# Order of the second network's mix units, and GpSimd casts for fourteen split rows, in an attention, maxout and PReLU kernel

## The chip, the cores and the metric

One Trainium2 chip, of which the kernel uses one core. The metric is device time in microseconds (us) of one execution. The kernel before was timed in three runs. One further execution was profiled, and all rows below come from that one. TensorE is called PE, VectorE DVE, ScalarE ACT, GpSimd POOL, and the engine that issues every DMA here is SyncE, SP.

## What is computed

```python
# attention: B, H, S, D = 4, 8, 576, 64; heads 0-3 see the last 32 positions, heads 4-7 every 32nd
attn = softmax(where(mask, q @ k.T / 8, -1e9)); x = (attn @ v) as rows        # (2304, 512)
h = maximum(maximum(x @ w1, x @ w2), x @ w3); x2 = h @ w_out                  # 512 -> 768 -> 512
h = x2 @ w_in; g = maximum(h, 0) + alpha * minimum(h, 0); out = g @ w_out2    # 512 -> 2048 -> 512
```

The texts call the first network (maxout) "the network" of a batch entry `b`: there are four, b = 0 to 3, each of 576 rows in two halves of 288 (`HALF`). "The second woven network" is that of b = 1. "The second net" of the diff's `split_x2`, the PReLU one, is called the output network here, to keep the two apart; it runs over three blocks of 768 rows, each in two parts of 384 (`HB`).

## The kernel before

All products run in fp32r as high part and low part: a value is cast to its high part and the rest becomes the low part (`split`, L236), and three matmuls replace one (`PAIRS`).

**Weave.** Attention for all four entries, the conversion of all weights and the networks of b = 0, 1, 2 are entered as tasks of a `Weave` (L53). A list planner on the host (`plan`) orders them: a task has a due position `pos`, what it needs, and ring buffers that it takes (8 PSUM banks, 10 tiles `x`, 4 tiles `t`, 12 tiles `h`); among the tasks that could start within 120 ns of the earliest on the engine that is free first, the one with the smallest position goes. The outcome is one fixed order of instructions for each engine. A network has 44 units on PE: 36 gate units of 12 matmuls (L752), three for each of six column groups and two halves, and 8 mix units of 18 matmuls (L777), four for each half. `units` turns a list into that order, and `net_tasks(b, list)` gives unit n the position 44 b + n. A mix unit needs the six `h` tiles of its half (high and low part), writes through one bank, an ACT copy (L823) and a `t` tile to DRAM (`store_x2`, L786). In a list, a pair is a group of three gate units and `None` stands for four mix units. The attention of entry b + 1 is woven under the network of b: scores (L358 local, L474 strided), transposes (L403, L523), values (L432, L547), whose results go into `x` tiles. The ring of `x` holds 10 tiles, an entry needs 8.

**Last network.** `last_net(3)` (from 291.5 us) is written out by hand. Twelve gate units come first, then 42 products of L932 (six groups k = 3 to 8 of seven, a Strassen-Winograd form) whose results DVE adds up (L912), one in seven being copied by ACT first (L950), then 8 mix units. In every third group (g = 2) each result gets a last maximum on DVE, an ACT cast (L945) and a DVE subtraction (L919) to become `h`.

**Early splits.** Block 1 of the output network needs 7 combinations of its rows for each of two halves of the columns, as high and low part in DRAM (`xd`). They are made inside `last_net`: step n of its loop emits `early_split` for n = 10, 12, ..., 22 (half 0) and n = 32, 34, ..., 44 (half 1). Each takes a tile of two pools of two buffers (`xst`, `xsu`, in turn), casts its 128x384 high part on ACT, subtracts on POOL (both L239/L242), and `early_store` issues the store at the step after. The sums that half 1 is split from are made by POOL (L1017, step 30), those of half 0 by DVE.

SP works its list in order: stores, then loads of the next factors (L865), of the rows of block 0 (`load_x2`, L1008, steps 45 and 47), of the output network's weights (L1060, L1072). DVE sums and splits block 0 (L1017, L242 at 354 to 366 us), and from 366.87 us PE runs the output network (L1401, L1202, L1208, L1212).

Due lists before:

```python
    GATES = [(0, 0), (0, 1), (0, 2), (1, 0), (0, 3), (0, 4), (1, 1), (0, 5), (1, 2),
             None, (1, 3), (1, 4), (1, 5), None]
    GATES_THEN = [what for what in GATES if what] + [None, None]
```

Of the kernel before, what the change touches and what calls it, by code (L numbers as in the profile page):

```python
# [57 lines left out]
class Weave:  # L58
# [16 lines left out]
    def add(self, engines, emit, pos, needs=(), gives=(), makes=(), uses=(), mode=None, slack=0, small=0):  # L75
        t = len(self.tasks)
        if engines[0][0] != "PE" and any(key in self.banks for key in uses):
            pos -= self.URGENT
        self.banks.update(key for ring, key in makes if ring == "bank")
        self.tasks.append((engines, emit, pos, needs, makes, mode, slack, small))  # L80
        for ring, key in makes:
            if ring in self.order:
                self.order[ring].append(key)
        for e in gives:
            self.givers.setdefault(e, []).append(t)
            if e[0] == "stored":
                self.stores.add(t)
        for key in [key for _, key in makes] + list(uses):
            self.users.setdefault(key, []).append(t)
# [89 lines left out]
def attention_maxout_prelu_kernel(  # L179
# [13 lines left out]
    nc = tc.nc  # L193
# [43 lines left out]
    def split(hi, lo, src, hi_engine, lo_engine):  # L237
        if hi_engine is nc.scalar:
            hi_engine.copy(hi, src)  # L239
        else:  # L240
            hi_engine.tensor_copy(hi, src)
        lo_engine.tensor_tensor(out=lo, in0=src, in1=hi.bitcast(F32), op=ALU.subtract)  # L242
# [5 lines left out]
    def pool(stack, name, bufs, side="left"):  # L248
        return stack.enter_context(tc.tile_pool(name=name, bufs=bufs, side=side, reuse_waits="tile"))
# [41 lines left out]
    def sub(out_, x, y):  # L291
        nc.vector.tensor_tensor(out=out_, in0=x, in1=y, op=ALU.subtract)  # L292

    def act(n, chip=False):
        return ("ACT", (50 if chip else 100) + 5 * n // 6)

    def dve(n, ops=1):
        return ("DVE", ops * (75 + 21 * n // 20))

    def load(kb):  # L300
        return (("SP", 3 * kb),)
# [443 lines left out]
    def gate_products(b, hf, f, g):  # L745
        acc = bank()
        unread(acc, UNREAD.get((b, hf, f, g), 0))
        acc = acc[:, :HALF]
        n = 0
        for cc in gate_order:  # L750
            for wi, xi in PAIRS:
                nc.tensor.matmul(acc, words["gate", f, g][:, wi, cc * P:(cc + 1) * P],  # L752
                                 xt[b, cc, hf][:, xi, :], start=n == 0, stop=n == 3 * NCC - 1)
                n += 1
        return acc
# [13 lines left out]
    def out1_products(b, hf, dc, st):  # L769
        acc = bank()[:, :HALF]  # L770
        out1_part(acc, hf, dc, st, range(NF1))
        return acc
# [7 lines left out]
    def store_x2(b, hf, dc, xo):  # L780
        first = b * S + hf * HALF
        done = 0
        while done < HALF:
            i, s = divmod(first + done, HB)
            nn = min(HALF - done, HB - s)
            nc.sync.dma_start(x2d[i][:, dc, s:s + nn], xo[:, done:done + nn])  # L786
            done += nn
# [3 lines left out]
    GATES_FIRST = [(0, 0), (0, 1), (1, 0), (0, 2), (1, 1), (0, 3), (1, 2), (0, 4), (1, 3), (0, 5),  # L791
                   (1, 4), None, (1, 5), None]
# [3 lines that stand above are left out]
    GATES_LAST = [(0, 0), (1, 0), (1, 1), (0, 1)]  # L796

    def units(gates):
        hf = 0
        for what in gates:  # L800
            if what is None:
                yield from ((hf, None, dc) for dc in range(NCC))
                hf += 1
            else:
                yield from ((*what, g) for g in range(3))

    def net_tasks(b, gates):
        sts = {}
        for n, (hf, f, g) in enumerate(units(gates)):
            pos = b * NUNITS + n  # L810
            u = (b, hf, f, g)
            ak = ("acc", u)
            if f is None:
                xok = ("xo", u)

                def products(_, hf=hf, dc=g, ak=ak, xok=xok):
                    tl[xok] = tp.tile([P, HALF], F32, tag="t", name="xo")
                    tl[ak] = out1_products(b, hf, dc, {("h", hf, f): tl["h", b, hf, f] for f in range(NF1)})

                hks = [("h", b, hf, f) for f in range(NF1)]  # L820
                add((("PE", 3 * NF1 * 132),), products, pos, needs=hks + [("mix", f) for f in range(NF1)],
                    gives=[ak], makes=[("bank", ak), ("t", xok)], uses=hks, mode="products")
                add((act(HALF, True),), lambda _, ak=ak, xok=xok: nc.scalar.copy(tl[xok], tl[ak]),  # L823
                    pos, needs=[ak], gives=[xok], uses=[ak, xok])
                add(load(144), lambda _, hf=hf, dc=g, xok=xok: store_x2(b, hf, dc, tl[xok]), pos,
                    needs=[xok], gives=[("x2", u)], uses=[xok])
                continue
            tk, hk = ("t", b, hf, f), ("h", b, hf, f)
            xks = [("x", b, cc, hf) for cc in range(NCC)]

            def products(_, hf=hf, f=f, g=g, ak=ak, tk=tk):
                if g == 0:
                    tl[tk] = tp.tile([P, HALF], F32, tag="t", name="t")
                tl[ak] = gate_products(b, hf, f, g)

            add((("PE", 3 * NCC * 132),), products, pos, gives=[ak, ("begun", g, tk)],
                needs=xks + [("gate", f, g)] + ([("begun", g - 1, tk)] if g else []),
                makes=[("bank", ak)] + ([("t", tk)] if g == 0 else []), uses=xks, mode="products")
            if g == 0:
                add((act(HALF, True),), lambda _, ak=ak, tk=tk: nc.scalar.copy(tl[tk], tl[ak]), pos,  # L840
                    needs=[ak], gives=[("t0", tk)], uses=[ak, tk])
            else:
                add((dve(HALF),), lambda _, ak=ak, tk=tk: nc.vector.tensor_tensor(  # L843
                    out=tl[tk], in0=tl[ak], in1=tl[tk], op=ALU.max), pos,
                    needs=[ak, (f"t{g - 1}", tk)], gives=[(f"t{g}", tk)], uses=[ak, tk])
            if g == 2:
                def high(_, tk=tk, hk=hk):
                    h = tl[hk] = hp.tile([P, 2, HALF], F32R, tag="x", name="h")
                    nc.scalar.copy(h[:, 0], tl[tk])

                add((act(HALF),), high, pos - 40, needs=[("t2", tk)], gives=[("hhi", hk)],
                    makes=[("h", hk)], uses=[tk])
                add((dve(HALF),), lambda _, tk=tk, hk=hk: sub(tl[hk][:, 1], tl[tk],
                                                              tl[hk][:, 0].bitcast(F32)),
                    pos - 40, needs=[("hhi", hk)], gives=[hk], uses=[tk, hk])

    def last_net(b):
# [130 lines left out]
        for hf in range(2):  # L988
            for dc in range(NCC):
# [9 lines left out]
    PRODUCTS = (((0, 0), "11"), ((2, 256), "T2"), ((0, 256), "21"), ((2, 0), "T3"),  # L999
                ((1, 0), "T1"), ((1, 256), "T4"), ((3, 0), "22"))  # L1000
    xs, x2h = {}, {}
# [22 lines left out]
                        ("T3", t3), ("T4", t4)):  # L1024
            xs[blk, name, i] = x

    def split_x2(blk, k, i, pool, tag, lo_engine=nc.vector):

        t = pool.tile([P, 2, HB], F32R, tag=tag, name=tag)
        split(t[:, 0], t[:, 1], xs.pop((blk, PRODUCTS[k][1], i)), nc.scalar, lo_engine)  # L1030
        return t

    early_rows, early_parts = {}, []
# [5 lines left out]
        sum_x2(blk, i, early_rows.pop((blk, i)), engine, later)  # L1039

    def early_split(blk, i, k, pool=None):
        early_parts.append((blk, k, i, split_x2(blk, k, i, pool or xst, "xst", nc.gpsimd)))

    def early_store():
        for blk, k, i, t in early_parts:
# [69 lines left out]
    for _, tasks, args in sorted(late, key=lambda it: it[0]):  # L1115
        tasks(*args)
    for b in range(B - 1):
        net_tasks(b, (GATES_FIRST, GATES, GATES_THEN)[b])
    weave.run()
    nc.sync.dma_start(alpha_sb, alpha)  # L1120
    conv_x.close()
# [4 lines left out]
    xst = pool(ctx, "xst", 2, "right")  # L1126
# [365 lines left out]
    for n in range(NQ * NBLK):  # L1492
        blk, q = divmod(n, NQ)
# [72 lines left out]
```

## Time and profile before

| | us |
|---|---|
| median of three runs | 726.78 |
| lowest and highest | 726.24, 728.15 |
| profiled execution | 727.66 |
| its span | 725.8 |
| outside the span (727.66 - 725.8) | 1.9 |

The profile gives busy time by engine, a table by stretch (busy time of each engine in a window of the span), the list of waits, the timeline of an engine (start and length of merged runs of equal instructions, with the idle time ahead of them and what ended it), the chain of waits (what the end of the program goes back to, piece by piece) and the DMAs (size, and time from issue to landing). A line such as `t<-bank,t` names what an instruction writes and reads. PE's ends are modelled, so a loss on PE is read from starts, and from the idle time in brackets.

### The profile page before, as it was taken

The page shows a single profiled execution, that of the slowest core. Times are in us where ns is not written, and L with a number is a line of the kernel's source. Part 1 is how long each engine was busy: PE and PEld are TensorE (multiplying, and loading weights), DVE is VectorE, ACT ScalarE, POOL GpSimd, SP SyncE. Part 2 cuts the span into 40 slices and gives each one's busy share as a digit, 9 for nine tenths or more (in the row PEclk, how much of TensorE's full clock was granted, in tenths as well). Part 3 has the DMA queues.
Part 4 walks back from the last instruction along what each step waited for, and adds up shares of the span by engine and source line. Part 5 has one row for each costly group of instructions (what it writes and reads, how often), then busy time and mean ns, then how long its engine had stood idle before and what let it go on. Part 6 is the DMA issues. An engine that isn't in the chain of part 4 may idle for free.

```text
span 725.8 us, 18183 instructions
## 1 busy us (share of the span) xinstructions
PE 714.3 (98%) x6682; PEld 696.4 (96%) x6682; DVE 619.1 (85%) x1689; ACT 443.2 (61%) x1175; POOL 25.6 (4%) x49
## 2 busy tenths in 40 slices
PE   8899999999999999999999999999999999999998
PEld 5799999999999999999999999999999999999997
DVE  6989886898989897679878988979988888888896
ACT  6879975977767484243356566535666644656561
POOL 2000000000000000045000000000000000000000
PEclk9999999999999999999999999999999999999999
DMA  8776599898999879698989899999789999878362
GB/s 298 268 259 229 174 334 314 312 315 307 345 339 324 279 250 321 204 351 294 326 322 400 274 330 340 403 386 360 245 301 329 372 402 344 295 233 259 113 190 77
DMA packets 90089, 214.46 MB, mean 295 GB/s; under 512 B 11152, under 2 KB 41360, under 8 KB 90000
## 3 DMA queue, kind: packets, MB, share of 16 engines
q1 hardware_dynamic: 90000, 213.30, 83.8%
q8 instruction: 53, 0.87, 0.5%
q14 instruction: 36, 0.29, 0.1%
HBM read 157.16 MB, written 56.10 MB: 294 GB/s over the span
## 4 chain that ended last, share of the span: by engine, by line
PE 92%; DMA 3%; ACT 2%; DVE 2%; issue 1%; POOL 0%; SPq 0%; DVEq 0%; POOLq 0%; ACTq 0%
PE bank L752 26%; PE ph L1401 24%; PE po L1202 15%; PE bank L777 10%; PE po L1208 4%; PE ph L1202 4%; PE po L1212 2%; PE bank L932 2%; PE bank L432 1%; DVE t L912 1%; DMA xd<-xst 1%; PE bank L358 1%; ACT e L374 1%; PE bank L474 1%; DMA w<-ws 1%; DMA k<-in_kTs 1%
## 5 line engine op out<-in xcount | busy, mean ns | idle before, releaser
L1401 PE MATMUL ph<-x,w 128*128 128x384 f32 x990 | 199.4, 336 | 0.0
L752 PE MATMUL bank<-x,w 128*128 128x288 f32 x1440 | 197.0, 297 | 1.2 <-ACT w L289 0.8
L752 PEld LDWEIGHTS bank<-x,w 128*128 128x128 f32 x1440 | 191.6, 189 | 2.7 <-ACT w L289 1.2
L1401 PEld LDWEIGHTS ph<-x,w 128*128 128x128 f32 x990 | 166.6, 188 | 0.8
L1202 PE MATMUL po<-w,g 128*128 128x256 f32 x936 | 135.9, 282 | 0.0
L1202 PEld LDWEIGHTS po<-w,g 128*128 128x128 f32 x936 | 130.1, 190 | 0.3
L1407 DVE TENSOR_TENSOR c<-ph,c 128x384 f32<-128x384 f32 x165 | 89.4, 554 | 30.6 <-PE ph L1401 29.9
L1195 ACT CAST g<-c 128x384 fp32r<-128x384 f32 x93 | 47.0, 505 | 90.7 <-DVE c L1385 51.6
L777 PE MATMUL bank<-h,w 128*128 128x288 f32 x576 | 79.9, 297 | 0.3 <-DVE h L919 0.2
L289 ACT CAST w<-word 128x512 fp32r<-128x512 f32 x100 | 57.8, 589 | 33.3 <-DMA wh<-w 10.1
L777 PEld LDWEIGHTS bank<-h,w 128*128 128x128 f32 x576 | 76.9, 189 | 1.0 <-DVE h L919 0.4
L292 DVE TENSOR_TENSOR w<-word,w 128x512 fp32r<-128x512 f32 x100 | 62.9, 642 | 16.5 <-ACT w L289 16.1
L1345 ACT ACTIVATE c<-c 128x384 f32<-128x384 f32 x96 | 50.6, 527 | 33.5 <-DVE c L1407 32.3
L1346 ACT ACTIVATE c<-c,nalpha 128x384 f32<-128x384 f32 x96 | 59.3, 618 | 3.1
L1350 DVE SCALAR_TENSOR_TENSOR c<-c 128x384 f32<-128x384 f32 x96 | 53.0, 552 | 5.9 <-ACT c L1346 5.9
L1196 DVE TENSOR_TENSOR g<-c,g 128x384 fp32r<-128x384 f32 x96 | 52.9, 551 | 0.9 <-ACT g L1195 0.5
L602 ACT ACTIVATE word<-raw 128x512 f32<-128x512 f32 x56 | 37.4, 679 | 12.4 <-DMA raw<-in_w 8.7
L1196 DVE TENSOR_TENSOR g<-k,g 128x384 fp32r<-128x384 f32 x72 | 37.1, 555 | 7.5 <-ACT g L1195 7.5
L1208 PE MATMUL po<-w,g 128*128 128x512 f32 x120 | 42.8, 396 | 0.0
L843 DVE TENSOR_TENSOR t<-bank,t 128x288 f32<-128x288 f32 x72 | 32.5, 452 | 6.3 <-PE bank L752 4.2
L1385 DVE TENSOR_TENSOR k<-c 128x384 f32<-128x384 f32 x72 | 37.9, 550 | 0.0
L1195 ACT CAST g<-k 128x384 fp32r<-128x384 f32 x72 | 33.1, 514 | 7.1 <-PE po L1208 3.3
(124 smaller groups left out, 896.0 us busy)
## 6 DMA issues: line engine op xcount, KB each, us to landing
w<-wh SPq DMA_DIRECT2D x72, 512.0 KB, 5.3
raw<-in_w SPq DMA_DIRECT2D x50, 512.0 KB, 5.4
w<-wo SPq DMA_DIRECT2D x48, 512.0 KB, 6.1
w<-wp SPq DMA_DIRECT2D x36, 512.0 KB, 5.7
wh<-w SPq DMA_DIRECT2D x24, 512.0 KB, 5.5
xd<-xst SPq DMA_DIRECT2D x28, 384.0 KB, 3.5
x<-xd SPq DMA_DIRECT2D x28, 384.0 KB, 8.1
ws<-w SPq DMA_DIRECT2D x12, 512.0 KB, 4.8
```

What stands on the lines that cost most here:

```text
L289: (nc.scalar.copy if e == "ACT" else nc.vector.tensor_copy)(out_, in_)
L292: nc.vector.tensor_tensor(out=out_, in0=x, in1=y, op=ALU.subtract)
L752: nc.tensor.matmul(acc, words["gate", f, g][:, wi, cc * P:(cc + 1) * P], xt[b, cc, hf][:, xi, :], start=n == 0, stop=n == 3 * NCC - 1)
L777: nc.tensor.matmul(acc, words["mix", f][:, wi, dc * P:(dc + 1) * P], st["h", hf, f][:, xi, :], start=f == n == 0, stop=f == NF1 - 1 and n ...
L1195: cast(g[:, 0], x)
L1196: return g, lambda: nc.vector.tensor_tensor(out=g[:, 1], in0=x, in1=g[:, 0].bitcast(F32), op=ALU.subtract)
L1202: nc.tensor.matmul(bank[:, NH * half:NH * (half + 1)], g[:, gi, t * P:(t + 1) * P], w[:, wi, off:off + NH], start=first and i == 0, stop=l ...
L1208: nc.tensor.matmul(bank.rearrange("p (s n) -> p s n", n=NH), g[:, 0, t * P:(t + 1) * P], w[:, :, off:off + NH], start=first, stop=last)
L1346: nc.scalar.activation(a, a, AF.Copy, scale=nalpha[:, f:f + 1])
L1350: nc.vector.scalar_tensor_tensor(out=a, in0=h, scalar=0.0, in1=a, op0=ALU.max, op1=ALU.add)
L1401: nc.tensor.matmul(bank, words["h", n, i][:, wi, off + c * P:off + (c + 1) * P], x2h[blk, k, c][:, xi, :], start=m == 0, stop=m == 5)
L1407: nc.vector.tensor_tensor(out=out_, in0=bank, in1=other, op=ALU.add)
```

## The change

1. `net_tasks(1, ...)` gets `GATES_THEN`, as b = 2 has already, for `GATES`: all twelve gate groups (36 units), then all eight mix units. Before, four mix units stood ahead of the last three groups. Nothing is added or taken away; the planner orders all tasks anew.
2. The fourteen early splits make the high part on POOL also. ACT loses fourteen 128x384 casts, POOL gets them; the subtraction stays on POOL. `split_x2` takes both engines now, and its other callers keep ACT and DVE.

```diff
-    def split_x2(blk, k, i, pool, tag, lo_engine=nc.vector):
+    def split_x2(blk, k, i, pool, tag, engines=(nc.scalar, nc.vector)):
 
         t = pool.tile([P, 2, HB], F32R, tag=tag, name=tag)
-        split(t[:, 0], t[:, 1], xs.pop((blk, PRODUCTS[k][1], i)), nc.scalar, lo_engine)
+        split(t[:, 0], t[:, 1], xs.pop((blk, PRODUCTS[k][1], i)), *engines)
         return t
...
-        early_parts.append((blk, k, i, split_x2(blk, k, i, pool or xst, "xst", nc.gpsimd)))
+        early_parts.append((blk, k, i, split_x2(blk, k, i, pool or xst, "xst", (nc.gpsimd, nc.gpsimd))))
...
-        net_tasks(b, (GATES_FIRST, GATES, GATES_THEN)[b])
+        net_tasks(b, (GATES_FIRST, GATES_THEN, GATES_THEN)[b])
```

## Rows read from the trace of the kernel before

**Rows 1.** The page's first part: busy us (share of the span) xinstructions.

```profile
PE 714.3 (98%) x6682; PEld 696.4 (96%) x6682; DVE 619.1 (85%) x1689; ACT 443.2 (61%) x1175; POOL 25.6 (4%) x49
```

**Rows 2.** Table by stretch: length, busy us by engine, granted clock, DMA share, GB/s.

```profile
310.00:352.00 42.00, 39.53 (x290) 38.53 (x289) 35.47 (x77) 13.03 (x32) 18.75 (x18) 1.00 0.93 334
...
367.00:700.00 333.00, 333.00 (x2239) 328.34 (x2238) 286.43 (x605) 191.40 (x389) 1.72 (x3) 1.00 0.88 315
```

**Rows 3.** PE's waits after 31 us: us in total, times, longest.

```profile
PE bank L932 <- ACT t L950: 2.2, 2, 1.2
PE bank L432 <- issue: 0.4, 1, 0.4
```

**Rows 4.** PE's timeline under the network of b = 1: start, length, what.

```profile
193.29 1.07 PE L432 MATMUL bank<-pt,v 64*64 64x32 f32 x37
...
195.46 7.40 PE L777 MATMUL bank<-h,w 128*128 128x288 f32 x54
```

**Rows 5.** PE's timeline, the same passage under the network of b = 0.

```profile
97.47 1.25 PE L432 MATMUL bank<-pt,v 64*64 64x32 f32 x72
98.65 0.62 PE L358 MATMUL bank<-k,q 64*32 64x64 f32 x36
```

**Rows 6.** PE's timeline in the last network.

```profile
323.73 11.60 PE L932 MATMUL bank<-x,w 128*128 128x288 f32 x84 [1.01 <-ACT t L950]
336.51 3.69 PE L932 MATMUL bank<-x,w 128*128 128x288 f32 x26 [1.18 <-ACT t L950]
```

**Rows 7.** ACT's timeline ahead of these two.

```profile
322.87 0.51 ACT L239 CAST xst<-xs 128x384 fp32r<-128x384 f32 x1 [4.95 <-DMA xd<-xst]
323.29 0.39 ACT L950 COPY t<-bank 128x288 f32<-128x288 f32 x1
...
335.32 0.43 ACT L945 CAST h<-t 128x288 fp32r<-128x288 f32 x1 [0.99 <-DVE t L912]
...
336.07 0.39 ACT L950 COPY t<-bank 128x288 f32<-128x288 f32 x1
```

**Rows 8.** Chain of waits, 310 to 324 us: start, length, what.

```profile
314.47 8.33 DMA xd<-xst
```

**Rows 9.** DVE's timeline in the last network.

```profile
323.71 1.02 DVE L912 TENSOR_TENSOR t<-bank,t 128x288 f32<-128x288 f32 x2 [3.23 <-ACT t L950]
...
341.40 1.36 DVE L912 TENSOR_TENSOR t<-t 128x288 f32<-128x288 f32 x1
...
350.92 0.45 DVE L919 TENSOR_TENSOR h<-t,h 128x288 fp32r<-128x288 f32 x1
```

**Rows 10.** DVE by line and shape, 323.6 to 346.2 us: busy, mean ns.

```profile
L912 DVE TENSOR_TENSOR t<-t 128x288 f32<-128x288 f32 x11 | 7.9, 719 | 0.3
L919 DVE TENSOR_TENSOR h<-t,h 128x288 fp32r<-128x288 f32 x4 | 2.9, 734 | 0.1
```

**Rows 11.** The same view, 346.3 to 353 us, when POOL is idle.

```profile
L912 DVE TENSOR_TENSOR t<-t 128x288 f32<-128x288 f32 x5 | 2.3, 458 | 0.1
```

**Rows 12.** POOL's timeline: last sum, two lows of half 1, two casts of a later stage.

```profile
337.41 1.12 POOL L1017 TENSOR_TENSOR t<-xs,t 128x384 f32<-128x384 f32 x1
...
341.41 1.02 POOL L242 TENSOR_TENSOR xst<-t,xst 128x384 fp32r<-128x384 f32 x1
...
344.83 1.02 POOL L242 TENSOR_TENSOR xst<-xs,xst 128x384 fp32r<-128x384 f32 x1 [0.23 <-ACT xst L239]
372.69 0.51 POOL L1195 CAST g<-c 128x384 fp32r<-128x384 f32 x1 [26.84 <-DVE c L1350]
...
376.36 0.70 POOL L1195 CAST g<-c 128x384 fp32r<-128x384 f32 x1 [0.83 <-DVE c L1350]
```

**Rows 13.** SP's timeline: loads of block 0's rows.

```profile
346.69 3.60 SPq L1008 DMA_DIRECT2D xs<-x  x4
```

**Rows 14.** DMA view, issues of 374.8 to 376.3 us: size, us to landing.

```profile
w<-wh SPq DMA_DIRECT2D x1, 512.0 KB, 8.6
```

**Rows 15.** PE's timeline, the output network's third step, first product.

```profile
385.71 1.21 PE L1401 MATMUL ph<-x,w 128*128 128x384 f32 x6
```

## The prediction

> **What bounds the kernel now.** First the page's busy times: PE is busy for 98% of the span, DVE for 85%, ACT for 61%, POOL for 4% [rows 1]. So a saving counts only where PE stands still, or does its work more slowly than elsewhere. Next the table by stretch: from 367 to 700 us PE is busy for the whole 333 us at a granted clock of 1.00 (2.4 GHz); from 310 to 352 us, the last network, it is busy for 39.5 of 42 us [rows 2]. Then PE's waits, which say where the loss lies: after 31 us there are two waits for an ACT copy, 2.2 us together, in the last network, and one of 0.4 us at the local values L432 [rows 3]. The change touches both places and no other loss on PE.
>
> **Part 1, the order under the network of b = 1.** The local values of one half are 72 short matmuls. Undisturbed they take 98.65 - 97.47 = 1.18 us from their start to the next work [rows 5]. In the middle network they took 195.46 - 193.29 = 2.17 us [rows 4]: 0.99 us are lost, of which only 0.40 stands as a wait. The reason is in the order. The last gate unit of b = 1 had just ended; the four mix units left are those of half 1, and they need the `h` that comes out of that gate unit by way of a DVE maximum, an ACT cast and a DVE subtraction; the gates of b = 2 need `x` tiles that these values have yet to make. PE has only the attention's short matmuls, whose inputs are copied just then. In the new list four mix units of half 0, ready long before, stand there, 72 matmuls. Under b = 0 mix units surround the same values, and nothing is lost there [rows 5].
> The cost: no instruction is added, and the other engines have the same work. The last four gate groups of b = 1 end four mix units earlier, so its `x` tiles come free earlier. What it could cost is a change of shape on PE more or less, or a new gap of the same kind, as the planner orders everything anew. The trace shows no gap elsewhere in the weave after 31 us [rows 3], so I bound that by one gap like this one: between -1.5 us (the gap and some changes of shape gone) and +0.8 us. I take -0.9: the 0.99 us, a little rounded down.
>
> **Part 2, what is removed from ACT.** At 322.87 us ACT starts a split's cast for which it has stood idle for 4.95 us, until a store of `xst` landed [rows 7]. That store took 8.33 us from issue, 314.47 to 322.80 [rows 8]. Behind the cast in ACT's order stands the copy L950 that frees a PSUM bank, at 323.29 us [rows 7]; PE waits 1.01 us for it and DVE 3.23 us [rows 6, 9]. With the cast on POOL, ACT copies as soon as PE has made the product, so this wait goes, and DVE's idle time with it. The second PE wait, 1.18 us ahead of 336.51 [rows 6], is the same copy again, now late since ACT waited for a DVE maximum (0.99 us ahead of 335.32) and then had a split's cast in front of the copy [rows 7]; DVE was late because of the 3.23 us. Both go, 2.2 us. After that PE is held by DVE: the product L777 at 351.42 starts when the second low part of `h`, made at 350.92 + 0.45 = 351.37 us, is there [rows 9].
>
> **Part 2, what is added to POOL.** Fourteen casts of 128x384; alone one takes 0.51 us, beside a DVE operation 0.70 [rows 12]. In half 0 the store still decides when the fifth tile is free, and by then POOL has nothing else. In half 1 POOL is the bound of its own chain: its sums end at 337.41 + 1.12 = 338.5 us, and its last low part at 344.83 + 1.02 = 345.85 [rows 12]. With seven pairs of cast and low part of about 1.5 us (0.51 + 1.02) that becomes 338.5 + 10.5 = 349.0, and with some 0.1 us for each of ten meetings with DVE 350. So POOL ends 4 us later.
> What does that cost DVE? A DVE operation with both inputs in SBUF waits while POOL works: that of 341.40 ended at 342.76, just after the POOL operation of 341.41 had ended at 342.43, and took 1.36 us [rows 9, 12]. While POOL is idle the same operation takes 0.458 us [rows 11]. In 323.6 to 346.2 us eleven maxima averaged 0.719 and four low parts 0.734 [rows 10], so the meetings cost 11 x 0.261 + 4 x 0.276 = 4.0 us, in about seven operations, 0.57 each. After the change about 13 such operations (four maxima in each of k = 4, 7 and 8, one low part) fall into POOL's time, and half of what they meet is a short cast. Bounds for one: 0.27 (a meeting at a random point of a cast or a low part, by the lengths above) and 0.57. So 3.5 to 7.4 us instead of 4.0; I take 13 x 0.42 = 5.5, that is 1.5 us more. DVE gains 3.2 us of idle time and gives 1.5 back: the second low part comes about 1.7 us earlier, at 349.7. PE without waits would arrive there 2.2 us earlier, so it waits for DVE a little longer than before, and goes on 1.7 us earlier. With the bounds, 0 to 2.2.
> The Trainium skill has a rule that speaks against the change: SBUF - State Buffer, section "SBUF: two separate sides", says that a DVE operation with two SBUF inputs and a GpSimd operation that reads SBUF take turns on one pair of ports, held for the whole instruction, whichever starts first. The trace agrees for low parts (1.36 us instead of 0.458); that a cast takes part in this, only the one of 0.70 us hints. If they did not, DVE would lose some 1 us less and the time would be about 0.5 us lower than I forecast, PE's own 2.2 us being the limit.
>
> **Part 2, the queue behind POOL.** SP stands behind POOL: its stores wait for the low parts, and behind them stand the loads of block 0's rows, first issued at 346.69 [rows 13], a moment after the last store. They move to about 350.4. Before, they were queued behind a run of stores (the DMA share of 310 to 352 us is 0.93 [rows 2]); with stores 1.5 us apart much of that queue is gone when they are issued, so I estimate that they land only 0.5 us later (bounds: 0, and the full 3.7). From these rows DVE and ACT make block 0's splits; ACT's bank copies and `x2` stores stand behind those, the output network's weights behind these on SP. The weight tile issued at 374.85 landed 8.6 us later, at 383.45 [rows 14], and PE first uses it at 385.71 [rows 15]: 2.26 us to spare. So part 2 can bring no more than 2.26 less the delay, 1.76 by my value, and with a delay of over 2.26 it costs. 1.7 just fits.
>
> **Sum.** -0.9 - 1.7 = -2.6; I take off 0.2 for the copy L950 of k = 6, which in this reckoning comes at the moment when PE needs its bank. So -2.4: from 727.66 us of the profiled execution to 725.3. Since from 367 us PE is never idle up to 700 [rows 2], what is gained stays. The profiled execution was 0.9 us over the median of 726.78; 2.4 less than that is **724.4 us**, 0.33% faster.
>
> **Rivals.**
> 1. *DVE pays all of it back.* With 0.57 for every meeting the extra is 3.4 us, as much as the idle time that goes, and part 2 brings 0 to 0.7 us. For it: all seven meetings before were that dear. Against: the new POOL operations are half as long. Time 726.78 - 0.9 - 0.4 = 725.5.
> 2. *POOL becomes the bound of the start of the output network: slower.* If its casts cost 0.9 to 1.0 us among DVE's operations and each low part 1.2, the seven pairs take over 15 us and POOL ends at 354 or later, 8 us later than before. The rows of block 0 then land 5 us later, PE waits for the weight tile for 5 - 2.26 = 2.7 us, and less the 0.9 of part 1 the time is 728.6. It decides from a delay of 2.26 + 0.9 = 3.2 us of those rows on. For it: the chain POOL, SP, ACT, SP, weights has no other slack. Against: the dearest cast seen is 0.70, and much of the delay is absorbed by a shorter DMA queue.
> 3. *Part 1 doesn't do what it says.* The planner follows readiness first and the list second; it may move the gap to another place, or make one: +0.5 instead of -0.9. Time 726.78 + 0.5 - 1.5 = 725.8.
> 4. *All of it.* Casts that hardly disturb DVE, rows that land no later, and changes of shape saved: -1.3 - 2.2 = -3.5, 723.3.
>
> **How the numbers follow.** Chances: forecast 0.45, rival 1 0.17, rival 2 0.11, rival 3 0.13, rival 4 0.14. About 0.3%, 2.2 us, is what a measurement of this kernel can tell from no change, so faster means under 724.6 and slower over 729.0. The forecast has its own range of 723.4 to 725.5, of which somewhat over half is under 724.6 (0.26); with rival 4 (0.14) and a part of rivals 1 and 3 (0.05) faster has 0.45. Slower has about 0.07: the larger part of rival 2 and a little of rival 3. The rest, 0.48, is within. The range takes in rival 4 below and rivals 1 and 3 above, with the part of rival 2 in which POOL is only somewhat late: 722.8 to 727.4.
>
> **What would show it.** Part 1: on PE's timeline 36 gate units in a row before any mix unit of b = 1, and 72 local values within 1.2 us. Part 2: no wait of L932 for L950, no DVE idle time near 320 us, POOL's last low part near 350, a maximum's mean still over 0.6 us there, PE resuming the mix about 1.7 us earlier relative to the start of the last network, and no wait of L1401 for `w` near 385. The prediction is wrong if PE waits for that tile, if the weave has a new gap of 1 us, or if the copy L950 is still late.

## The result, and the profile after

The changed kernel took 732.67 us (median of four runs, 731.60 to 733.38) beside 727.46 us for the kernel before on the same chip: a ratio of 1.0065, with a 95% interval of 1.0041 to 1.0088. It is slower by more than the 0.3% that can be told from no change, and outside the forecast's range. The profiled execution took 733.38 us, its span 5.7 us more than that of before.

The page of the kernel after, its first part, which answers to [rows 1]:

```profile
PE 716.7 (98%) x6682; PEld 698.2 (95%) x6682; DVE 618.0 (84%) x1687; ACT 438.2 (60%) x1163; POOL 35.4 (5%) x63
```

POOL has its fourteen casts and 9.8 us more work, ACT some 5 us less. None of PE's waits in [rows 3] is left. The last network has two short new ones, 0.22 and 0.43 us, for low and high parts of `x` ahead of L932 at 311.19 and 314.12 us, and the start of the output network has three.

PE's timeline of the kernel after (start, length, what, and in brackets the idle time ahead of it with what ended it). The first two rows answer to [rows 4], the last to [rows 15]:

```profile
188.11 1.25 PE L432 MATMUL bank<-pt,v 64*64 64x32 f32 x72
189.29 7.39 PE L777 MATMUL bank<-h,w 128*128 128x288 f32 x54
...
345.36 19.23 PE L777 MATMUL bank<-h,w 128*128 128x288 f32 x144
364.43 0.69 PE L1401 MATMUL ph<-x,w 128*128 128x384 f32 x3
365.74 0.45 PE L1401 MATMUL ph<-x,w 128*128 128x384 f32 x1 [0.62 <-ACT x L239]
368.77 0.62 PE L1401 MATMUL ph<-x,w 128*128 128x384 f32 x2 [2.58 <-DVE x L242]
370.91 2.29 PE L1401 MATMUL ph<-x,w 128*128 128x384 f32 x6 [1.52 <-ACT xo L995]
373.00 3.89 PE L1401 MATMUL po<-x,w 128*128 128x384 f32 x12
376.73 2.25 PE L1401 MATMUL ph<-x,w 128*128 128x384 f32 x12
...
391.41 1.21 PE L1401 MATMUL ph<-x,w 128*128 128x384 f32 x6
```

The same place in the kernel before, where no wait is shown:

```profile
366.87 2.25 PE L1401 MATMUL ph<-x,w 128*128 128x384 f32 x12
368.96 2.24 PE L1401 MATMUL po<-x,w 128*128 128x384 f32 x12
```

Up to 364.43 us the time came out nearly as forecast: PE reaches the output network 2.44 us earlier than the 366.87 of before. By the third step's first product it is 5.70 us late (391.41 against 385.71 in [rows 15]), which is the whole difference of the spans. So 2.44 + 5.70 = 8.14 us are lost between these two points, and nothing anywhere else. The table by stretch of the kernel after (length; busy us of PE, PEld, DVE, ACT, POOL; granted clock; DMA share; GB/s) shows two kinds of loss:

```profile
364.00:370.00 6.00, 2.19 (x11) 1.28 (x9) 5.90 (x13) 4.00 (x11) 0.00 (x0) 0.98 0.48 162
370.00:377.00 7.00, 6.09 (x20) 6.09 (x21) 2.81 (x8) 3.38 (x9) 0.00 (x0) 0.53 0.89 300
377.00:391.00 14.00, 14.00 (x93) 14.00 (x92) 12.71 (x27) 7.97 (x15) 1.71 (x3) 1.00 1.03 405
```

From 364 to 370 us PE stands still for 3.8 us while DVE is busy throughout. From 370 to 377 us PE is busy nearly always, but at a granted clock of 0.53, that is nearly all the time at 1.2 GHz. Before, from 367 us on, it was 1.00 [rows 2].

What made PE wait? POOL's timeline of the kernel after, two casts of half 0 and then half 1 from its sums on, and SP's at the loads of block 0's rows (answering to [rows 12, 13]); then DVE's first sum of those rows and the low part that PE waited for; last, DVE's first sum in the kernel before:

```profile
320.27 0.50 POOL L241 CAST xst<-xs 128x384 fp32r<-128x384 f32 x1
...
321.80 0.50 POOL L241 CAST xst<-t 128x384 fp32r<-128x384 f32 x1
...
335.92 1.01 POOL L1017 TENSOR_TENSOR t<-xs 128x384 f32<-128x384 f32 x1 [6.93 <-DMA xs<-x]
...
340.34 0.50 POOL L241 CAST xst<-xs 128x384 fp32r<-128x384 f32 x1
340.92 1.10 POOL L242 TENSOR_TENSOR xst<-xs,xst 128x384 fp32r<-128x384 f32 x1
341.97 0.73 POOL L241 CAST xst<-t 128x384 fp32r<-128x384 f32 x1
342.78 1.29 POOL L242 TENSOR_TENSOR xst<-t,xst 128x384 fp32r<-128x384 f32 x1
...
352.26 1.01 POOL L242 TENSOR_TENSOR xst<-xs,xst 128x384 fp32r<-128x384 f32 x1
```

```profile
353.67 1.94 SPq L1008 DMA_DIRECT2D xs<-x  x4
```

```profile
360.27 0.56 DVE L1017 TENSOR_TENSOR t<-xs 128x384 f32<-128x384 f32 x1 [8.45 <-DMA xs<-x]
...
368.17 0.55 DVE L242 TENSOR_TENSOR x<-xst,x 128x384 fp32r<-128x384 f32 x1
```

```profile
354.11 0.56 DVE L1017 TENSOR_TENSOR t<-xs 128x384 f32<-128x384 f32 x1 [0.56 <-DMA xs<-x]
```

An undisturbed pair of cast and low part, here one of half 0, takes 321.80 - 320.27 = 1.53 us; in half 1 a pair takes 1.85 on the mean. POOL's last low part ends at 352.26 + 1.01 = 353.27 us instead of 345.85. SP, which stands behind it with a store, issues the rows of block 0 at 353.67 instead of 346.69. DVE, idle for 8.45 us, can sum them from 360.27 instead of 354.11. PE's wait of 2.58 us ends at 368.77 with the low part that DVE began at 368.17. The wait for `xo` behind it is for a bank copy that stands behind the same splits in ACT's order. ACT's timeline, first of the kernel before, then of the kernel after:

```profile
365.21 1.00 ACT L995 COPY xo<-bank 128x288 f32<-128x288 f32 x3
```

```profile
370.47 1.39 ACT L995 COPY xo<-bank 128x288 f32<-128x288 f32 x4
```

The copies come 5.26 us later, and they are what decides. Before, the first of these copies was done at about 365.21 + 0.39 = 365.6; PE wanted the bank for its seventh matmul at 366.87 + 6 x 0.174 = 367.91 (twelve matmuls took 368.96 - 366.87 = 2.09 us there). That is a margin of 2.3 us. Now the copy is 5.26 us later and PE is 2.44 us earlier: 5.26 + 2.44 - 2.31 = 5.39. The seventh matmul begins at 370.91 instead of 364.43 + 1.04 = 365.47, which is 5.44 us. The other 2.70 us of the 8.14 lie behind it, where nothing waits: six matmuls in 373.00 - 370.91 = 2.09 us (0.35 each) and twelve in 3.73 us (0.31 each), against 0.174 before. That is the half clock.

### The profile page after: what moved, and what is told of

Read it like the earlier page. It is cut to its first block, busy times and chain, and to the rows that moved or that the text cites. A ratio compares the mean times of both kernels' runs of the same rounds, so it can differ in the third digit from the quotient of the medians.

```text
span 731.5 us, 18172 instructions
## 1 busy us (share of the span) xinstructions
PE 716.7 (98%) x6682; PEld 698.2 (95%) x6682; DVE 618.0 (84%) x1687; ACT 438.2 (60%) x1163; POOL 35.4 (5%) x63
## 4 chain that ended last, share of the span: by engine, by line
PE 85%; DVE 4%; ACT 3%; DMA 3%; POOL 2%; issue 1%; SPq 1%; ACTq 0%; DVEq 0%; POOLq 0%
PE ph L1401 24%; PE bank L752 23%; PE po L1202 15%; PE bank L777 8%; PE po L1208 4%; PE ph L1202 4%; PE po L1212 2%; DVE t L912 1%; PE bank L432 1%; POOL xst L242 1%; PE bank L358 1%; DMA xst<-x 1%; ACT e L374 1%; PE bank L474 1%; DMA k<-in_kTs 1%
```

## The experiments

Each was compared with runs of the kernel before on the same chip; ratios are to those, with 95% intervals. "New order" is part 1, "casts on POOL" is part 2. The diffs are cut to the lines that matter, "..." marks what is left out; unless said otherwise they are edits of the kernel after.

**The two parts alone.** New order, casts on ACT as before (an edit of the kernel before):

```diff
-        net_tasks(b, (GATES_FIRST, GATES, GATES_THEN)[b])
+        net_tasks(b, (GATES_FIRST, GATES_THEN, GATES_THEN)[b])
```

> Only the order under the network of b = 1 is changed; the casts stay on ACT. Theory T (the loss comes from GpSimd's longer chain alone, through the rows of block 0 that are loaded behind it; the new order brings its 0.7 to 0.9 us): 0.5 to 1 us faster than before, the output network's first product without a wait, clock 1.00 throughout. Rival O (the new order leaves a longer tail of weight conversion at the end of the weave, and this delays the last network and what follows): 1 to 3 us slower than before.

Measured: 1.0004 (0.9987 to 1.0021), 727.68 us; span 724.8. Old order, casts on POOL:

```diff
-        net_tasks(b, (GATES_FIRST, GATES_THEN, GATES_THEN)[b])
+        net_tasks(b, (GATES_FIRST, GATES, GATES_THEN)[b])
```

> Only the casts are moved to GpSimd; the order is the old one. Theory T: nearly the whole loss, 4.5 to 6.5 us slower than before, with waits of 3 to 5 us ahead of the output network's first products and a stretch at clock 0.5 behind them. Rival O: less than 3 us slower, since half of the lateness would be the new order's.

Measured: 1.0085 (1.0055 to 1.0114), 734.79 us; span 734.4. So the loss is part 2's, all of it, and part 1 alone shows no difference in the time. PE's timeline at the start of the output network, first of the order alone, then of the casts alone:

```profile
365.58 2.35 PE L1401 MATMUL ph<-x,w 128*128 128x384 f32 x12 [0.64 <-ACT xo L995]
```

```profile
372.83 4.21 PE L1401 MATMUL ph<-x,w 128*128 128x384 f32 x12 [4.91 <-ACT xo L995]
```

With the casts alone PE waits 4.91 us, and 12 matmuls take 4.21 us instead of 2.25. With the order alone it waits 0.64 us. One thing besides the edit differs here: in these two programs (and in that with POOL casts for half 0, below) PE is held once, ahead of the output network's first matmul, where the kernel after and the kernel before with POOL delayed (below) are held ahead of the fourth, fifth and seventh. So the order alone gives 0.64 us back that it may otherwise have kept.

The kernel before was profiled once more, for the gap at the local values:

> The kernel before once more, for a second profile, since its executions differ by several us. If the loss at the local values of the middle network (0.99 us in the first profile) is the order's, it stands here too, 0.5 us or more. If it was one execution's, PE goes on to the mix units within 1.3 us of the first local value here, and the new order had nothing to give.

Its time was 731.15 us. PE's timeline of that profile:

```profile
197.19 1.07 PE L432 MATMUL bank<-pt,v 64*64 64x32 f32 x37
198.89 0.77 PE L432 MATMUL bank<-pt,v 64*64 64x32 f32 x35 [0.63 <-issue]
```

All four profiles with the old order have an idle stretch there (0.40, 0.63, 1.16 and 1.48 us), none of the nine with the new one has. From the first gate unit (24.76 us in before) to the last network's start (291.52), the four took 266.8 to 269.6 us, the nine 265.9 to 266.3. So the gap and its removal are shown; a gain in the time is not (the interval reaches from -0.13% to +0.21%, and 0.9 us would be 0.12%).

The mean granted clock that each timed execution has on record says one thing more. In the kernel before it was 0.998 or less in 34 of the 82 executions that the experiments were compared with, and these took 1.9 to 3.3 us longer, by the medians on each chip, than the others. With the order alone it was so in 1 of 12, with the order and block 0's rows sooner (below) in none of 12. The executions above 0.998 show no gain from the order: 727.52 us with it alone, the 0.64 us included, and 726.03 before on that chip. Where the clock fell in the executions without a profile is not shown. The second profile of before has 3.4 us at half clock from about 13.5 us on, behind a wait of 1.95 us for a load; in the first the clock stayed at 1.00.

**Is lateness alone enough?** The kernel before, with work added to POOL that nobody needs, ahead of the last low part:

```diff
+        if lo_engine is nc.gpsimd and (i, k) == (1, 6):
+            for _ in range(19):
+                nc.gpsimd.memset(t[:, 1].bitcast(F32), 0.0)
```

> The kernel before with 19 memsets of 128x384 on GpSimd ahead of the last low part of half 1: they read nothing and compute nothing that is used, and move only the end of GpSimd's chain, by some 7 us; ACT and the order are as before. Theory T (the end of GpSimd's chain sets when block 0's rows can be loaded, and these when the output network can start): 1.5 to 5 us slower than before, with waits ahead of the output network's first products as in the changed kernel. Rival P (GpSimd's operations cost through the ports and the casts, not through the queue behind them): within 0.5 us of before.

Measured: 1.0117 (1.0094 to 1.0139), 735.66 us. POOL's and PE's timelines and the table by stretch of this kernel:

```profile
345.56 8.99 POOL L1032 MEMSET xst<- 128x384 f32 x19
```

```profile
367.84 0.44 PE L1404 MATMUL ph<-x,w 128*128 128x384 f32 x1 [1.31 <-ACT x L239]
371.29 1.01 PE L1404 MATMUL ph<-x,w 128*128 128x384 f32 x2 [3.02 <-DVE x L242]
373.43 2.29 PE L1404 MATMUL ph<-x,w 128*128 128x384 f32 x6 [1.13 <-ACT xo L995]
```

```profile
370.00:377.00 7.00, 4.58 (x13) 4.07 (x14) 4.66 (x11) 4.55 (x12) 0.00 (x0) 0.51 0.53 153
```

ACT makes the casts here, as before; only POOL's end moved, to 355.65 us. The same three waits for the same three things come, and the same half clock. A late POOL is enough for the loss; neither the casts' contention with DVE nor the new order is needed for it. The loss is more than the 1.5 to 5 us expected: 1.17% is 8.5 us. POOL's end moved by 9.8 us and not by 7, and in the profile 2.4 us lie in the weave, ahead of the delay, where the gap at the local values was 1.16 us and the clock stood at one half for 3.4 us behind it.

This profile shows one thing more. PE has no wait at all in the last network, though ACT stands behind the store of `xst` as it did before. ACT's timeline, of the kernel with POOL delayed, of the second profile of before, and of the order alone (answering to [rows 7]):

```profile
322.52 0.51 ACT L239 CAST xst<-xs 128x384 fp32r<-128x384 f32 x1 [2.94 <-DMA xd<-xst]
```

```profile
326.59 0.51 ACT L239 CAST xst<-xs 128x384 fp32r<-128x384 f32 x1 [4.31 <-DMA xd<-xst]
```

```profile
321.48 0.51 ACT L239 CAST xst<-xs 128x384 fp32r<-128x384 f32 x1 [3.60 <-DMA xd<-xst]
```

ACT stood idle for 4.95 us in the profiled execution of before, and PE lost 1.01 + 1.18 = 2.2 us [rows 6, 7]. With 4.31 us PE lost 0.47 + 0.94, with 3.60 us 0.20 + 0.62, with 2.94 us nothing. How long ACT stands there differs from execution to execution, and what part 2 can win of it lay between 0 and 2.2 us in these five profiles.

**Does the loss go when the rows come sooner?** The changed kernel, with half 1's splits that read `xs` tiles put ahead of those that read `t` tiles, so that block 0's rows can be loaded six steps sooner into the tile that comes free. POOL's work is the same:

```diff
-    ready = {X_SPLIT + 22 * half + 2 * k: (1, half, k) for half in range(2) for k in range(7)}
+    ready = {X_SPLIT + 22 * half + 2 * j: (1, half, k) for half in range(2)
+             for j, k in enumerate((range(7), (0, 4, 2, 6, 1, 3, 5))[half])}
...
-        if n == gates - 9:
+        if n == gates - 15:
             rows = [load_x2(0, 0, xsp, "xs")]
```

> The whole change, but half 1's splits go in the order 11, T1, 21, 22, T2, T3, T4, so that the tiles of its rows are free after the fourth, and the loads of block 0's first rows are issued behind the fourth store and not behind the seventh. GpSimd does the same work. Theory T: the rows land 4 to 5 us earlier than in the changed kernel, the wait ahead of the output network shrinks to under 1 us and no slow clock follows: 1 us slower to 2 us faster than before. Rival P: 4 to 6 us slower than before, as the whole change.

Measured: 1.0030 (1.0015 to 1.0044), 729.57 us. PE's timeline:

```profile
365.54 0.62 PE L1402 MATMUL ph<-x,w 128*128 128x384 f32 x2 [1.49 <-DVE x L242]
367.68 2.29 PE L1402 MATMUL ph<-x,w 128*128 128x384 f32 x6 [1.52 <-ACT xo L995]
```

The first rows land at 355.18 us instead of 360.14, the second part at 362.60 instead of 365.08; PE waits 3.0 us instead of 4.7, and half of the loss is gone. The half clock stays. The same edit with the casts on ACT and the new order:

> The new order alone, casts on ACT, with the same new order of half 1's splits and earlier loads of block 0's rows. Theory T with its second part (the start of the output network is held by these rows in the kernel before too, so that a gain ahead of it turns into a wait): the wait of 0.6 us ahead of the output network that the new order alone showed goes: 0.5 to 2 us faster than the new order alone, so 0 to 1.5 us faster than before. If the rows are not the bound there: as the new order alone, within 0.4 us.

Measured: 0.9994 (0.9981 to 1.0007), 726.61 us: no wait at the output network, no half clock, and no measurable gain over before either; in its last network PE waits 0.17 + 0.61 us again with ACT's casts back, and 0.79 + 0.23 us among the first mix units.

**What does the half clock cost?** Matmuls whose results nobody reads, into the unused columns of a bank, fill PE's wait: 46 in the changed kernel, 30 in the one with the rows sooner:

```diff
+        whole = [ps_h.tile([P, DM], F32, tag="ph", name="ph") for _ in range(2)]
+        banks = [t[:, :HB] for t in whole]
...
+                for _ in range(46 * (n == k == 0 and c == 1)):
+                    nc.tensor.matmul(whole[1][:, HB:], words["h", 0, 0][:, 0, :P], x2h[0, 0, 0][:, 0, :P],
+                                     start=False, stop=False)
```

> The whole change, and 46 matmuls of 128 columns, whose results nobody reads, between the two halves of the output network's first product, where TensorE stands waiting for block 0's rows. They fill some 3 to 5 us of its idle time and change nothing else. If the stretch at half clock that follows the wait is a cost of its own and comes from the idle time: no such stretch, and 2 to 3.5 us faster than the whole change. If it isn't (the clock falls anyway, or the loss is the wait alone): as the whole change, within 1 us, or slower by what the matmuls take.

> The changed kernel with half 1's splits reordered and block 0's first rows loaded sooner (two waits of 1.5 us were left there, and 6.8 us at half clock behind them), and 30 such matmuls of 128 columns in that place. If idle time brings the half clock: clock 1.00, some 3 us faster than without them, so 1 us slower to 1 us faster than before.

Measured: 1.0048 (1.0025 to 1.0071) and 1.0010 (0.9992 to 1.0029). PE's timeline and the table by stretch of the first:

```profile
363.98 5.24 PE L1402 MATMUL ph<-x,w 128*128 128x128 f32 x46
369.06 0.74 PE L1405 MATMUL ph<-x,w 128*128 128x384 f32 x3
370.27 1.31 PE L1405 MATMUL ph<-x,w 128*128 128x384 f32 x6 [0.47 <-ACT xo L995]
```

```profile
370.00:377.00 7.00, 6.73 (x39) 6.74 (x40) 5.18 (x12) 3.98 (x10) 0.50 (x1) 1.00 0.93 321
```

The matmuls that need the second part of the rows resume at nearly the same time as without the filling (369.06 against 368.77), but at a clock of 1.00. From the output network's first product to the third step's first it is 24.71 us instead of 26.98, and in the second pair 22.55 instead of 25.13: the half clock costs 2.3 to 2.6 us in the profiles. In the runs both pairs move the same way (-0.17% and -0.20%, 1.2 and 1.5 us), but each pair's intervals overlap. The twelve runs of the rows-sooner kernel give the size once more: in nine the mean clock was 0.995 or 0.997 and the median 729.84 us, in three 0.999 or 1.00 and 727.63, which is 2.2 us (though those three may have waited less too).

**Casts on POOL for half 0 only, and for the last three of each half only**, to keep ACT's gain and shorten POOL's chain:

```diff
+        high = nc.scalar if i else nc.gpsimd
-        early_parts.append((blk, k, i, split_x2(blk, k, i, pool or xst, "xst", (nc.gpsimd, nc.gpsimd))))
+        early_parts.append((blk, k, i, split_x2(blk, k, i, pool or xst, "xst", (high, nc.gpsimd))))
```

> The whole change, but half 1's seven casts back on ACT, so that GpSimd has casts for half 0 alone. Theory T: GpSimd's last low part back at 346 to 348 us, no wait ahead of the output network, the gain of the last network kept: 1.5 to 3 us faster than before. Rival P (what hurts is that GpSimd's operations block VectorE's in the last network): only half of the loss gone, 2 to 3 us slower than before. Rival O: 0 to 2 us slower than before.

```diff
+        high = nc.gpsimd if k > 3 else nc.scalar
...
```

> The whole change, but in each half only the last three casts (those that wait for a buffer, so that ACT never stands behind a store) are on GpSimd, the first four on ACT. A smaller dose of the suspected cause: GpSimd's chain of half 1 is some 2 to 3 us longer than before instead of 7. Theory T: the rows land 1 to 2 us later than before and just in time: 1 to 2.5 us faster than before. Rival P: 1 to 3 us slower than before.

Measured: 1.0022 (1.0004 to 1.0041) and 1.0011 (0.9993 to 1.0029). Neither keeps the gain. ACT's timeline, first of half 0 only, then of the last three:

```profile
344.35 0.51 ACT L239 CAST xst<-xs 128x384 fp32r<-128x384 f32 x1 [2.82 <-DMA xd<-xst]
...
347.45 0.39 ACT L950 COPY t<-bank 128x288 f32<-128x288 f32 x1
```

```profile
337.80 0.51 ACT L239 CAST xst<-t 128x384 fp32r<-128x384 f32 x1 [3.99 <-POOL t L1017]
```

In the first, ACT stands behind a store again, now in half 1. PE waits 0.67 us for a copy L950 behind a cast that was held by the load of half 1's rows (at 335.9 us), and 0.79 us for an `h` cast that itself waited for DVE. In the second ACT stands 3.99 us for POOL's sum with the copy L950 behind it. ACT's casts stall wherever what they wait for is late; a part of them left there brings the stall back. POOL ends at 348.6 and 348.4 us in them; at the output network PE waits 0.54 us in the first and not at all in the second, and most of part 2's loss is gone. The second has a half clock all the same, in the last network, behind four waits of PE for `h` (0.29, 0.31, 0.79 and 0.23 us within 3 us; table by stretch):

```profile
351.00:354.50 3.50, 3.50 (x17) 3.50 (x18) 1.74 (x5) 1.67 (x4) 0.00 (x0) 0.57 0.93 296
```

**POOL's chain earlier altogether.** The rows-sooner kernel, with the rows of half 1 fetched six steps sooner and the `xs` readers first in both halves:

```diff
+             for j, k in enumerate((0, 2, 6, 4, 1, 3, 5))}
...
-            if n == X_SPLIT + 21 * half - 8:
+            if n == (X_SPLIT - 8, X_SPLIT + 7)[half]:
                 early_load(1, half, xsp, "xs")
```

> The whole change, and the splits of both halves in the order 11, 21, 22, T1, T2, T3, T4, the loads of half 1's rows behind the fourth store of half 0, and those of block 0's first rows behind the fourth store of half 1. GpSimd has the same work, but three splits start before the sums are made, and the sums of half 1 follow half 0 at once. Theory T: GpSimd ends some 8 us earlier than in the changed kernel, no wait ahead of the output network, clock 1.00, and the gain of the last network is kept: 2 to 4 us faster than before. If the ports are what limits GpSimd's use (its operations now meet VectorE's earlier): 0 to 3 us slower than before.

Measured: 0.9994 (0.9974 to 1.0015), 727.58 us. PE's timeline:

```profile
336.03 1.05 PE L932 MATMUL bank<-x,w 128*128 128x288 f32 x6 [0.43 <-DVE t L912]
337.60 10.68 PE L932 MATMUL bank<-x,w 128*128 128x288 f32 x78 [0.52 <-ACT t L950]
...
367.18 2.25 PE L1402 MATMUL ph<-x,w 128*128 128x384 f32 x12
```

POOL ends at 345.49 us, the output network starts without a wait at full clock: the loss is cured. But PE reaches it at 367.18, not 364.43. POOL's work now lies where each product has its last maximum, and DVE's maxima there average 672 ns (line and shape, 323.6 to 352 us: busy, mean ns), against 596 ns in the kernel after:

```profile
L912 DVE TENSOR_TENSOR t<-t 128x288 f32<-128x288 f32 x16 | 10.8, 672 | 0.4
```

PE waits five times (0.70, 0.28, 0.18, 0.43, 0.52 us) in the last network. In this profile what the casts give at one end they take at the other. No version tried is measurably faster than the kernel before.

## Why the prediction was wrong

- **What bounds the kernel** held for PE in the last network, but not at its end. The prediction took PE's uninterrupted work from 367 us [rows 2] to mean that what is gained ahead of it stays. The row says only that nothing was late; the bank copies had 2.3 us to spare and no more.
- **Part 1** was right in the profile: the local values take 189.29 - 188.11 = 1.18 us as under b = 0, and the weave from first gate unit to the last network 265.90 us instead of 266.76, that is -0.86 against -0.9. The other engines did not keep quite the same work: with the new order alone DVE has two instructions fewer and ACT two more (x1687 and x1177 instead of x1689 and x1175). A gain in time is not shown.
- **Part 2, what is removed from ACT**, was right: no wait for L950, no idle DVE near 320 us. The sum up to the output network came out, 2.44 us gained against 2.6, but by luck. Of these 1.77 us are part 2's (35.47 instead of 36.41 us for the products, 19.07 instead of 19.90 for the mix units), where 1.7 were forecast, with DVE as the limit: PE was to wait for it a little longer than before. In the kernel after PE doesn't wait for DVE at the mix at all. The waits of 1.01, 1.18 and 0.23 us are gone, 2.42 together, and the two new ones of 0.22 and 0.43 us ahead of them take 0.65 back. Besides, the 2.2 us were one execution's: four other profiles with the casts on ACT lost 0 to 1.4 us where this one lost 2.2, so part 2 had less to win than the rows of one execution said.
- **Part 2, POOL's contention with DVE (rival 1)**, was over-priced. DVE by line and shape in the kernel after, 323 to 352 us (answering to [rows 10]):

```profile
L912 DVE TENSOR_TENSOR t<-t 128x288 f32<-128x288 f32 x16 | 9.5, 596 | 0.4
L919 DVE TENSOR_TENSOR h<-t,h 128x288 fp32r<-128x288 f32 x8 | 5.0, 634 | 0.3
```

That is 16 x 0.138 + 8 x 0.18 = 3.6 us over the 0.458 us of an undisturbed operation [rows 11], less than the 4.0 before, where 5.5 were forecast. The lock that the Trainium skill describes (SBUF — State Buffer, section "SBUF: two separate sides") makes the later one wait; here POOL was often the later one: its casts took 0.50 or 0.73 us and more, and its low parts 1.01 or up to 1.30. So what the casts added was paid not by DVE but as a longer chain on POOL.
- **Part 2, the queue behind POOL, is the step that failed**, in three terms. *POOL's end:* 353.27 us, not 350. Half 1's work started 1.85 us later (half 0's last low part ended at 328.99 instead of 326.63, half 1's rows landed 2 us later), where the prediction let the store decide and took nothing; and seven pairs took 353.27 - 340.34 = 12.93 us, 1.85 each, where it took 11.5. *What the queue absorbs:* rows issued 6.98 us later landed 6.15 us later; the prediction let 3.7 us shrink to 0.5, because the DMA share was 0.93. A busy queue did not mean that an earlier issue was worthless. *The limit:* the prediction set the slack by a weight tile, 2.26 us. That tile, issued at 378.87 us in the kernel after, landed 8.3 us later, at 387.2, and was used at 391.41: it had 4.2 us to spare (DMA view, answering to [rows 14]).

```profile
w<-wh SPq DMA_DIRECT2D x1, 512.0 KB, 8.3
```

What ran out were block 0's own splits and the bank copies behind them on ACT. Their 2.3 us would have been used up by the 2.44 us that PE gained, without any delay. None of the three signs that the prediction named for being wrong came: no wait for the tile, no new gap in the weave, no late copy L950.
- **The half clock** was no term of the sum: 2.3 to 2.7 us.
- **Rival 2** was the true case, given 0.11: POOL at 353.3 (it said 354), the rows 6.2 us later (it said 5). It named the wrong last link, and its price was too low: 5 - 2.26 = 2.7 us less 0.9, where the copies' delay of 5.26, in which what part 1 brings is counted already, less 2.31 makes 2.95 us, and the clock adds 2.70: 5.65 of the 5.70 us. Its "for" (no other slack in the chain) did not hold: the rows landed 6.15 us later, the weight tile only 3.75 (387.20 against 383.45). Of its two "against" the first held, the dearest cast of half 1 took 0.74 us and the seven pairs 12.9 and not over 15; POOL was late all the same, by the later start. The second fell, the queue absorbed 0.8 us.

What stays open: which part of DVE's and POOL's delays is whose, operation by operation; and whether part 1's 0.9 us are in the time, which is less than these intervals can tell; and where the clock falls in those executions of the kernel before that have no profile.

## What to carry to other kernels

When work is moved onto an engine that a DMA queue waits for, follow the queue behind that engine up to the next stage's first inputs, and subtract from their slack also what the bounding engine gains, since it arrives earlier. An uninterrupted busy stretch says nothing of how late its inputs may be: read that from the last producers' ends against their use. Price a helper engine's chain under contention (here 1.85 us a pair instead of 1.53). Starting that chain earlier cured the late queue here, but put its work beside more of DVE's, and the time was that of before.

## What the runs showed of the hardware

- TensorE's granted clock fell to 1.2 GHz (0.5) for 6.8 us around 3.0 to 5.5 us of waits at the output network, in one piece (casts alone) or in two or three (the kernel after, rows sooner, POOL delayed). It fell for 3.4 us after 1.16 and 1.48 us of idle time among the 64x32 matmuls of the local values (POOL delayed, casts alone), after 1.62 us of waits in four pieces (casts on POOL for the last three), and after one wait of 1.95 us for a load near 12 us (second profile of before). Single waits of 1.01 and 1.18 us [rows 6], and one of 1.61 us in the second profile of before, left it at 1.00. In the kernel after, the clock costs 2.70 us behind 5.44 us of delay by the waits. The Trainium skill (TensorE: Matmul & The Clock Gate, section "HAM oscillation — how this bites in real kernels") says that waits for data throttle the array, so that the work behind them starts at half rate, and advises to order the work so that it stays fast; the 46 filling matmuls, with 1.00 instead of 0.53 from 370 to 377 us, agree.
- A one-input cast of 128x384 on POOL took 0.50 us alone and mostly 0.73 beside DVE's two-input operations (0.82 once), and a low part 1.01 or 1.10 to 1.31, in the kernel after: the seven pairs of half 1 lost 7 x (1.85 - 1.53) = 2.2 us to that.
